# Turning 32x32 diagonal blocks on the vector engine in place of two trips through DRAM, in a DeltaNet and mixer kernel

## The chip, the cores and the metric

The kernel runs on one core of a Trainium2 chip. The metric is the time of one execution on that core in microseconds (us), as the median of several executions. A run is called faster or slower when it differs by more than 2%, and unclear when the interval reaches across that line. Every ratio quoted below is the mean time of one kernel's runs over the mean time of the other kernel's runs of the same rounds, so it is not quite the ratio of the medians that stand beside it. The kernel before has two medians below: 850.98 us from its first three runs, 851.62 with a fourth.

Engine names in the profile: PE is TensorE (matmuls), DVE is VectorE, ACT is ScalarE, POOL is GpSimd, SP is SyncE, which issues most DMAs. The *granted clock* is the TensorE clock allowed in a stretch, as the profile gives it, as a share of full speed (0.50 to 1.00 in the windows of the prediction). An *eviction* is the copy that takes a matmul's result out of its accumulator, and a *hole* is a long stretch in which PE stands idle.

## The reference

```python
# q, k, v: (4, 8, 768, 48); beta: (4, 8, 768)
k_n = k / (norm(k) + 1e-6)
for t in range(S):                               # DeltaNet, per batch and head
    y[t]  = q[t] @ state
    v_old = k_n[t] @ state
    state = state + beta[t] * outer(k_n[t], v[t] - v_old)
# then, per batch, a mixer on x = (768, 384):
u   = x + (relu(x.T @ w_tok1) @ w_tok2).T
out = u + relu(u @ w_ch1) @ w_ch2
```

The kernel does the recurrence in chunks of 64 tokens. In each chunk the chain of updates becomes a triangular 64x64 system for each head, and its inverse is built from two 32x32 diagonal blocks and one block between them.

## The kernel before

A *unit* is 128 tokens of one batch (two chunks, eight heads, so 16 triangular systems); there are 24 units, six for each batch. For a unit, `prep` makes the masked products `gm`. Its 32 diagonal 32x32 blocks (two for each system) lie with the row on the partition. `invert` wants one whole block on each partition, so that VectorE can invert up to 128 blocks at once by 60 small instructions (0.37 us each in the trace). The change of layout goes through DRAM, out and back. A *round* is the set of units inverted together; there are seven. The code counts them from zero, so "rounds two and later" are the third to the seventh; they are called the later rounds here. `join` completes the 64x64 inverse and `recur` walks the chunks.

```python
rounds = [[0, 1], [2, 3, 4, 5]]                  # then four units each

def prep(u):
    ...                                          # transposes, kqt and kbd copies
    for g in range(2):                           # p_g: key-query products
        ...
        nc.vector.tensor_tensor(out=gm[:, r, 0::2], in0=p_g, in1=mb..., op=ALU.mult)
    for par in range(2):                         # first trip, out
        for i in range(2):
            nc.sync.dma_start(
                out=xins[rnd][lo : lo + NB].rearrange("b s t -> s b t"),
                in_=gm[row : row + HB, :, 2, HB * i : HB * i + HB])

def invert(rnd):
    nc.sync.dma_start(out=x, in_=xins.pop(rnd)[0:n])         # first trip, back
    for s in range(1, HB - 1):
        nc.vector.tensor_tensor(out=tmp, ..., op=ALU.mult)
        nc.vector.tensor_tensor(out=x[:, 0:s, s + 1 : HB], ..., in1=tmp, op=ALU.add)
    nc.vector.memset(...)                                    # ones on the diagonal
    nc.sync.dma_start(out=w_dram[0:n], in_=x)                # second trip, out

def fetch_w(u):                                              # second trip, back
    nc.sync.dma_start(out=wt[row : row + HB, :, HB * i : HB * i + HB],
                      in_=w_dram[lo : lo + NB].rearrange("b s t -> s b t"))

def join(u):
    nc.vector.transpose(t11[...], wt[r, :, 0:HB])
    ...  # p_z = gm block x t11, copied to zst; p_x = zst x wt, copied into wt

def recur(t):
    # p_q = s_bd x kqt      -> r_bd = v - p_q  (VectorE)
    # p_w = wt x r_bd       -> w_bd            (ScalarE)
    # p_s = gm x w_bd       -> s_bd, y         (VectorE)
    ...
```

A plan gives every piece of work a time, and the instructions are emitted in that order, so each engine's stream is fixed when the kernel is built. The build still reorders a little: e5 below keeps the plan, and yet its instructions run in another order on every engine. The mixer of a batch runs beside the recurrence of the next.

## Time and profile before

| quantity | before |
|---|---|
| median time | 850.98 us (850.45 to 856.06) |
| span in the trace | 850.4 us |
| first p_z (first join) | 84.9 us |
| first matmul of the first mixer | 202.2 us |
| from there to the end | 648.2 us |
| busy share PE, DVE, ACT | 86%, 46%, 30% |

How to read it: the first matmul of the mixer (out `p`, in `xb` and `w`) divides the span. Before it, PE waits for the preparation; after it, PE is almost full (busy 490.45 of the 500.40 us from 350 us on) and the recurrences of the later batches run between mixer matmuls. I use two numbers: the *mixer start* and the *rest*. They add up to the span.

The prediction shows the slices, the windows and the waits before the mixer start. One more view is needed later: what PE waited for *after* it, on behalf of the recurrence. The columns of a wait line are the waiting engine and matmul, what ended the wait, the us in all, the number of waits, and the longest. Kernel before, waits of PE in 202.2 to 850.4 us:

```profile
PE p_z L413 <- DVE t L407: 3.2, 3, 2.3
PE p_q L453 <- DVE s_bd L486: 2.5, 2, 1.5
PE p_w L470 <- DVE r_bd L455: 1.6, 3, 0.6
```

With two further waits (0.4 us for p_z, 0.2 us for p_s) that is 7.9 us in 648: the later rounds, with their DRAM trips, stand almost entirely beside other work.

### The profile page before, as it was taken

To read this page: it belongs to the slowest core of one execution; us is meant where nothing else is said; L and a number is where in the kernel's file an instruction comes from. 1 tells how busy PE (TensorE), PEld (TensorE's weight loads), DVE (VectorE), ACT (ScalarE), POOL (GpSimd) and SP (SyncE) were. 2 spreads that over 40 slices of the span, in tenths; PEclk is the share of its full clock that TensorE was granted. 3 is DMA by queue.
4 is the path that set the end of the run, shared out by engine and by line. 5 is a ranking of instruction groups with operands and counts; after the bars stand their busy time and mean duration, and the time that the engine had idled before them with its cause. 6 is when DMAs were issued, how large, how long until landed. Compare 5 with 4: busy or idle time off the path is not lost.

```text
span 850.4 us, 13384 instructions
## 1 busy us (share of the span) xinstructions
PE 732.3 (86%) x5080; PEld 606.6 (71%) x5080; DVE 394.8 (46%) x1081; ACT 253.0 (30%) x596; POOL 111.6 (13%) x142
## 2 busy tenths in 40 slices
PE   5630654969689999999999899999999999999998
PEld 4620644856469797887787888886898888678876
DVE  4487775756973459333267323493229422010000
ACT  5430422744234522333231333311332222111110
POOL 4322112223430211002000001110000000000000
PEclk9765755987899999999999999999999999999999
DMA  7763414445433441224122223202110200000000
GB/s 137 138 144 63 107 28 126 71 82 155 121 109 53 71 94 24 68 44 78 29 48 54 43 49 69 46 19 53 22 39 20 44 11 10 9 1 20 11 9 19
DMA packets 164591, 49.73 MB, mean 58 GB/s; under 512 B 155536, under 2 KB 158608, under 8 KB 164528
## 3 DMA queue, kind: packets, MB, share of 16 engines
q1 hardware_dynamic: 164480, 48.79, 26.6%
q8 instruction: 40, 0.66, 0.3%
q14 instruction: 23, 0.19, 0.1%
q10 hardware_dynamic: 48, 0.10, 0.0%
HBM read 37.85 MB, written 11.01 MB: 57 GB/s over the span
## 4 chain that ended last, share of the span: by engine, by line
PE 49%; DVE 9%; DMA 2%; ACT 2%; issue 1%; SPq 1%; ACTq 0%
PE p_c L549 16%; PE p_o L564 15%; DVE x L377 3%; DVE sub L373 3%; PE p_h L523 3%; PE p_s L482 2%; PE p_g L338 2%; PE p_q L453 2%; PE p L510 2%; PE p_w L470 2%; PE p_x L422 1%; PE p_z L413 1%; SPq L251 1%; PE p_ut L533 1%; DMA kst<-in_k_dram 1%
## 5 line engine op out<-in xcount | busy, mean ns | idle before, releaser
L549 PE MATMUL p_c<-u_t,wc 128*128 128x128 f32 x1728 | 218.2, 280 | 2.5 <-ACT u_t L537 1.8
L549 PEld LDWEIGHTS p_c<-u_t,wc 128*128 128x128 f32 x1728 | 206.5, 195 | 7.8 <-ACT u_t L537 2.5
L564 PE MATMUL p_o<-wc,r 128*128 128x384 f32 x576 | 197.5, 490 | 3.1 <-DVE wc L195 3.1
L564 PEld LDWEIGHTS p_o<-wc,r 128*128 128x128 f32 x576 | 105.0, 191 | 64.8 <-DVE wc L195 4.4
L556 ACT ACTIVATE r<-p_c 128x512 f32<-128x512 f32 x72 | 43.0, 597 | 156.8 <-PE p_c L549 156.4
L373 DVE TENSOR_TENSOR sub<-x 128x84 f32<-128x84 f32 (+22 forms) x210 | 77.3, 368 | 22.9 <-DMA x<-n_dram 18.3
L377 DVE TENSOR_TENSOR x<-x,sub 128x84 f32<-128x84 f32 (+22 forms) x210 | 76.7, 365 | 4.7
L338 PE MATMUL p_g<-kqt,kbd 128*128 128x128 f32 x384 | 60.1, 313 | 17.9 <-ACT kqt L326 17.7
L413 PE MATMUL p_z<-t,gm 128*65 128x64 f32 x384 | 30.7, 236 | 50.2 <-DVE t L407 49.8
L338 PEld LDWEIGHTS p_g<-kqt,kbd 128*128 128x128 f32 x384 | 55.1, 223 | 24.0 <-ACT kqt L326 22.5
L570 DVE TENSOR_TENSOR xb<-xb,p_o 128x384 f32<-128x384 f32 x24 | 13.3, 554 | 116.2 <-PE p_o L564 116.0
L413 PEld LDWEIGHTS p_z<-t,gm 128*65 128x65 f32 x384 | 28.7, 151 | 52.7 <-issue 28.5
L486 DVE TENSOR_TENSOR s_bd<-s_bd,p_s 64x192 f32<-64x192 f32 (+1 forms) x100 | 31.6, 316 | 73.9 <-PE p_s L482 72.2
L482 PE MATMUL p_s<-w_bd,gm 128*128 128x96 f32 x384 | 58.5, 297 | 5.2 <-ACT w_bd L474 4.9
L482 PEld LDWEIGHTS p_s<-w_bd,gm 128*128 128x128 f32 x384 | 52.6, 208 | 10.3 <-ACT w_bd L474 9.1
L340 DVE TENSOR_TENSOR gm<-p_g,mb 128x512 f32<-128x512 f32 x48 | 33.0, 690 | 57.3 <-PE p_g L338 55.0
L453 PE MATMUL p_q<-s_bd,kqt 128*128 128x96 f32 x352 | 50.9, 287 | 4.2 <-DVE s_bd L486 3.9
L453 PEld LDWEIGHTS p_q<-s_bd,kqt 128*128 128x128 f32 x352 | 47.1, 201 | 9.6 <-issue 3.0
L470 PE MATMUL p_w<-r_bd,wt 128*65 128x96 f32 x384 | 45.5, 263 | 7.2 <-issue 3.5
L455 DVE TENSOR_TENSOR r_bd<-v_st,p_q 64x192 f32<-64x192 f32 (+1 forms) x110 | 34.8, 316 | 35.1 <-PE p_q L453 23.0
L459 ACT ACTIVATE xb<-p_q 64x384 f32<-64x384 f32 (+1 forms) x55 | 23.0, 419 | 92.7 <-DVE r_bd L455 92.4
L474 ACT COPY w_bd<-p_w 64x192 f32<-64x192 f32 (+1 forms) x120 | 33.5, 280 | 54.0 <-PE p_w L470 52.0
(70 smaller groups left out, 708.8 us busy)
## 6 DMA issues: line engine op xcount, KB each, us to landing
d<-in_moe_w_ch_dram SPq DMA_DIRECT2D x24, 384.0 KB, 3.3
kpad<-in_k_dram SPq DMA_DIRECT2D x24, 192.0 KB, 3.5
kst<-in_k_dram SPq DMA_DIRECT2D x96, 48.0 KB, 2.6
qpad<-in_q_dram SPq DMA_DIRECT2D x24, 192.0 KB, 3.6
v_st<-in_v_dram SPq DMA_DIRECT2D x96, 48.0 KB, 2.6
out_dram<-xb SPq DMA_DIRECT2D x24, 192.0 KB, 1.9
n_dram<-gm SPq DMA_DIRECT2D x96, 32.0 KB, 1.7
wt<-w_dram SPq DMA_DIRECT2D x96, 32.0 KB, 2.1
```

The lines of the kernel that those rows point to most:

```text
L338: nc.tensor.matmul(p_g[:, i], kbd[:, nb], kqt[:, nb])
L373: nc.vector.tensor_tensor(out=tmp, in0=x[:, 0:s, s : s + 1].to_broadcast([n, s, w]), in1=x[:, s : s + 1, s + 1 : HB].to_broadcast([n, s, w ...
L377: nc.vector.tensor_tensor(out=x[:, 0:s, s + 1 : HB], in0=x[:, 0:s, s + 1 : HB], in1=tmp, op=ALU.add,)
L413: nc.tensor.matmul(p_z[0:65, nb], gm[:, lo : lo + 65], t11[:, nb])
L453: nc.tensor.matmul(p_q[:, p], kqt[:, 2 * p + cc], s0[:, p])
L455: nc.vector.tensor_tensor(out=r_bd[r, hp, e], in0=v_st[r, hp, cc], in1=p_q[hi, hp, e], op=ALU.subtract,)
L470: nc.tensor.matmul(p_w[0 : C + 1, p], wts[u % NW][:, w_lo : w_lo + C + 1], r_bd[:, p])
L474: nc.scalar.copy(w_bd[r, hp, e], p_w[lo, hp, e])
L482: nc.tensor.matmul(p_s[:, p], gm[:, 2 * p + cc, 0:2], w_bd[:, p])
L549: nc.tensor.matmul(p_c[:, i], wc1[:, cb, f * 128 : (f + 1) * 128], u_t[:, cb], start=(cb == 0), stop=(cb == NCB - 1),)
L556: nc.scalar.activation(r, p_c, ACTF.Relu)
L564: nc.tensor.matmul(p_o, r2[f // FG][:, f % FG], wc2[:, f], start=(f == 0), stop=(f == NHT - 1),)
```

## The change

The intent: do the change of layout on the chip. Four copies a unit put the diagonal blocks into a `turned` tile, one VectorE instruction (STREAM_TRANSPOSE in the trace, 1.97 us for 128x1024) transposes its 32x32 blocks, and the inverse comes back the same way into the place of the masked block in `gm`. With that, the first round takes four units, so that one long wait for an inversion goes away.

```diff
-    rounds = [[0, 1], [2, 3, 4, 5]]
+    rounds = [[0, 1, 2, 3], [4, 5]]
 ...
+    turned = const.tile([128, HB, RU * NB], FP32, name="turned")
 # prep(u), at its end
-                nc.sync.dma_start(out=xins[rnd][...].rearrange("b s t -> s b t"), in_=gm[...])
+        for block, t in quarters(u):
+            nc.scalar.copy(t, block)
 # quarters(u): for the four 32-row quarters r
+            yield (gm_of(u)[r, :, 2, cols],
+                   turneds[rnd][r, :, lo : lo + NB].rearrange("s t b -> s b t"))
 # invert(rnd)
-        nc.sync.dma_start(out=x, in_=xins.pop(rnd)[0:n])
+        nc.vector.transpose(x.rearrange("b s t -> b t s"), turned)
 ...
-        nc.sync.dma_start(out=w_dram[0:n], in_=x)
+        nc.vector.transpose(turned, x.rearrange("b s t -> b t s"))
+        for u in rounds[rnd]:
+            for i, (block, t) in enumerate(quarters(u)):
+                if u < NCH and i % 2:
+                    nc.vector.tensor_copy(out=block, in_=t)
+                else:
+                    nc.scalar.copy(block, t)
-    def fetch_w(u): ...                          # gone, with the wt tiles
 # the key loads of the first four units move from SyncE's to ScalarE's queue
-                stacked(kst, k, u)
+                stacked(kst, k, u, nc.scalar if u < NK else nc.sync)
 # plan of the first round
-                at(-3.5 + 0.3 * j, 0.06, prep, u)
+                at(-3.7 + 0.3 * j, 0.06, prep, u)
 ...                                              # and of the inversions
```

Cut: a scaling moved from GpSimd to VectorE in the first round, a fourth key buffer, the load of beta moved to SyncE, the in-place square in the weight rounding, merged tiles, a second `turned` tile borrowed for the second round, and the other plan times. Note the layout of `turned`: index `t` outside, block index inside. A copy of one unit's quarter therefore writes (or reads) one element in every 32, a step of 128 bytes.

More of the change, by code (lines that the diff above doesn't have):

```diff
@@ L80 @@
     )
-    dram = ctx.enter_context(
-        tc.tile_pool(name="dram", bufs=2, space=bass.MemoryType.DRAM)
-    )
     def ps_prep(shape, name):
@@ L112 @@
     NV = 6
-    NW = 3
-    NK = 3
+    NK = 4
     kpad = tiles("kpad", [128, H, DP], NK)
@@ L120 @@
     GW = 3 * DP
-    gms = tiles("gm", [128, NB * GW + 8], NV)
+    gm_all = const.tile([128, NV * NB * GW + 8], FP32, name="gm")
+    gmb = gm_all[:, 0 : NV * NB * GW].rearrange("s (b n) -> s b n", n=GW)
     kqts = tiles("kqt", [128, NB, 2, C], NV)
     nrms = tiles("nrm", [128, NP, 2], NV)
-    wts = tiles("wt", [128, NB * C + 8], NW)
-    t11s = tiles("t11_", [128, NB, 2 * HB], 2)
+    t11 = const.tile([128, NB, 2 * HB], FP32, name="t11")
+    turned = const.tile([128, HB, RU * NB], FP32, name="turned")
     zst = const.tile([128, NB * 2 * HB + 8], FP32, name="zst")
@@ L136 @@
     nc.vector.memset(kbd, 0.0)
-    for t in gms:
-        pad = t[:, 0 : NB * GW].rearrange("s (b three n) -> s b three n", b=NB, n=DP)
-        nc.vector.memset(pad[:, :, 1, D:DP], 0.0)
-        nc.gpsimd.memset(t[:, NB * GW :], 0.0)
-    for t in t11s + wts + [zst]:
+    nc.vector.memset(gmb[:, :, DP + D : 2 * DP], 0.0)
+    nc.gpsimd.memset(gm_all[:, NV * NB * GW :], 0.0)
+    for t in [t11, zst, turned]:
         nc.gpsimd.memset(t, 0.0)
@@ L155, in load_beta @@
         rows = mlp_pool.tile([B * H, S], FP32, name="b_rows", tag="xb")
-        nc.scalar.dma_start(out=rows, in_=beta.rearrange("b h s -> (b h) s"))
+        nc.sync.dma_start(out=rows, in_=beta.rearrange("b h s -> (b h) s"))
         yield
@@ L181, in round_weights @@
         f = loads.tile([128, WP], U32, name="w_f")[:, 0:n]
-        a = loads.tile([128, WP], FP32, name="w_a")[:, 0:n]
         nc.scalar.activation(lo, lo, ACTF.Copy, scale=2.0**-29)
-        nc.scalar.square(a, hi.bitcast(FP32))
         nc.vector.tensor_scalar(
@@ L192, in round_weights @@
         )
+        a = hi.bitcast(FP32)
+        nc.scalar.square(a, a)
         nc.gpsimd.tensor_tensor(out=f, in0=f, in1=lo, op=ALU.add)
@@ L218 @@
     ksts = {}
-    xins = {}
-    xouts = {}
-    rounds = [[0, 1], [2, 3, 4, 5]]
+    rounds = [[0, 1, 2, 3], [4, 5]]
     while rounds[-1][-1] < NU - 1:
@@ L226 @@
     turning = set()
+    masked = set()
+    inverted = set()
     walked = set()
@@ L237, in load_kq @@
         b, c = divmod(u, NCH)
-        ksts[u] = kst = loads.tile([128, NP, 2, D], FP32, name="kst")
+        ksts[u] = kst = loads.tile([128, NP, 2, D], FP32, name="kst", bufs=NK)
         for pad, src in ((kpad, k), (qpad, q)):
@@ L244, in load_kq, with stacked @@
             if src is k:
-                stacked(kst, k, u)
-    def stacked(dst, src, u):
+                stacked(kst, k, u, nc.scalar if u < NK else nc.sync)
+    def stacked(dst, src, u, queue):
         rows = heads_of(src, u)
@@ L250, in stacked @@
             for cc in range(2):
-                nc.sync.dma_start(
+                queue.dma_start(
                     out=dst[C * par : C * par + C, :, cc], in_=rows[par, cc]
@@ L256, in load_v @@
         vsts[u] = v_st = loads.tile([128, NP, 2, D], FP32, name="v_st")
-        stacked(v_st, v, u)
+        stacked(v_st, v, u, nc.sync)
         yield
@@ L270, in gm_of, with weights_of @@
     def gm_of(u):
-        return gms[u % NV][:, 0 : NB * GW].rearrange(
-            "s (b three n) -> s b three n", three=3, n=DP
-        )
-    def wt_of(u):
-        return wts[u % NW][:, 0 : NB * C].rearrange("s (b n) -> s b n", n=C)
+        return gmb[:, (u % NV) * NB : (u % NV + 1) * NB].rearrange(
+            "s b (three n) -> s b three n", n=DP
+        )
+    def weights_of(u, nb):
+        lo = ((u % NV) * NB + nb) * GW + 2 * DP
+        return gm_all[:, lo : lo + C + 1]
     def prep(u):
@@ L316, in prep @@
         mb = work.tile([128, NP, 2, C], FP32, name="mb", bufs=1)
-        nc.gpsimd.tensor_tensor(
+        scaler = nc.vector if u in rounds[0] else nc.gpsimd
+        scaler.tensor_tensor(
             out=mb, in0=mask_c[:, None, None, :].to_broadcast([128, NP, 2, C]),
@@ L326, in prep @@
         nc.scalar.mul(kqt_q, p_t, -1.0)
-        nc.gpsimd.tensor_tensor(
+        scaler.tensor_tensor(
             out=gm[:, :, 1, 0:D].rearrange("s (p c) d -> s p c d", c=2), in0=kst,
@@ L347, in prep, with turn_for, quarters @@
             yield
+        if round_of[u][1] == 0:
+            turn_for(round_of[u][0])
+        for block, t in quarters(u):
+            nc.scalar.copy(t, block)
         turning.remove(u)
-        rnd, j = round_of[u]
-        if j == 0:
-            xins[rnd] = dram.tile([RU * 4 * NB, HB, HB], FP32, name="n_dram")
-        for par in range(2):
-            for i in range(2):
-                lo = (4 * j + 2 * par + i) * NB
-                row = C * par + HB * i
-                nc.sync.dma_start(
-                    out=xins[rnd][lo : lo + NB].rearrange("b s t -> s b t"),
-                    in_=gm[row : row + HB, :, 2, HB * i : HB * i + HB],
-                )
-        yield
-    def invert(rnd):
-        n = 4 * NB * len(rounds[rnd])
-        x = work.tile([RU * 4 * NB, HB, HB], FP32, name="x", bufs=1)[0:n]
-        nc.sync.dma_start(out=x, in_=xins.pop(rnd)[0:n])
+        masked.add(u)
+    turneds = {}
+    def turn_for(rnd):
+        if rnd == 1:
+            turneds[rnd] = mlp_pool.tile([128, HB, RU * NB], FP32, name="xb", tag="xb")
+            nc.gpsimd.memset(turneds[rnd], 0.0)
+        else:
+            assert not set(turneds) - {1}
+            turneds[rnd] = turned
+    def quarters(u):
+        rnd, j = round_of[u]
+        lo = j * NB
+        for i in range(4):
+            r = slice(HB * i, HB * i + HB)
+            cols = slice(HB * (i % 2), HB * (i % 2) + HB)
+            yield (
+                gm_of(u)[r, :, 2, cols],
+                turneds[rnd][r, :, lo : lo + NB].rearrange("s t b -> s b t"),
+            )
+    def invert(rnd):
+        n = 128
+        assert masked.issuperset(rounds[rnd])
+        turned = turneds[rnd]
+        x = work.tile([n, HB, HB], FP32, name="x", bufs=1)
+        nc.vector.transpose(x.rearrange("b s t -> b t s"), turned)
         yield
@@ L370, in invert @@
             w = HB - 1 - s
-            tmp = work.tile([RU * 4 * NB, HB * HB // 4], FP32, name="sub")
+            tmp = work.tile([n, HB * HB // 4], FP32, name="sub")
             tmp = tmp[0:n, 0 : s * w].rearrange("b (s w) -> b s w", w=w)
@@ L382, in invert @@
         nc.vector.memset(x.rearrange("b s t -> b (s t)")[:, 0 :: HB + 1], 1.0)
-        xouts[rnd] = w_dram = dram.tile([RU * 4 * NB, HB, HB], FP32, name="w_dram")
-        nc.sync.dma_start(out=w_dram[0:n], in_=x)
-        yield
-    def fetch_w(u):
-        assert u < NW or u - NW in walked
-        rnd, j = round_of[u]
-        w_dram, wt = xouts[rnd], wt_of(u)
-        for i in range(2):
-            for par in range(2):
-                lo = (4 * j + 2 * par + i) * NB
-                row = C * par + HB * i
-                nc.sync.dma_start(
-                    out=wt[row : row + HB, :, HB * i : HB * i + HB],
-                    in_=w_dram[lo : lo + NB].rearrange("b s t -> s b t"),
-                )
+        nc.vector.transpose(turned, x.rearrange("b s t -> b t s"))
[3 more added lines that the diff above has]
+                    nc.vector.tensor_copy(out=block, in_=t)
+                else:
+                    nc.scalar.copy(block, t)
+        del turneds[rnd]
+        inverted.update(rounds[rnd])
+        yield
     def join(u):
-        gm, wt = gms[u % NV], wt_of(u)
-        t11 = t11s[u % 2]
+        assert u in inverted
+        wt = gm_of(u)[:, :, 2]
         for par in range(2):
@@ L411, in join @@
         for nb in range(NB):
-            lo = nb * GW + 2 * DP
-            nc.tensor.matmul(p_z[0:65, nb], gm[:, lo : lo + 65], t11[:, nb])
+            nc.tensor.matmul(p_z[0 : C + 1, nb], weights_of(u, nb), t11[:, nb])
         z = zst[:, 0 : NB * 2 * HB].rearrange("s (b n) -> s b n", n=2 * HB)
@@ L468, in recur @@
             for p in range(p0, p1):
-                w_lo = (2 * p + cc) * C
                 nc.tensor.matmul(
-                    p_w[0 : C + 1, p], wts[u % NW][:, w_lo : w_lo + C + 1], r_bd[:, p]
+                    p_w[0 : C + 1, p], weights_of(u, 2 * p + cc), r_bd[:, p]
                 )
@@ L610 @@
             if rnd == 0:
-                at(-3.5 + 0.3 * j, 0.06, prep, u)
+                at(-3.7 + 0.3 * j, 0.06, prep, u)
             elif rnd == 1:
-                at(-2.7 + 0.4 * j, 0.06, prep, u)
+                at(-1.9 + 0.7 * j, 0.12, prep, u)
             else:
                 at(max(t0 - 3.0 + 0.3 * j, start(u - NV + 1) + 0.01), 0.06, prep, u)
-            at(start(u) - 0.45, 0, fetch_w, u)
             at(start(u) - 0.3, 0.1, join, u)
         if rnd == 0:
-            at(-2.7, 2.0 / (HB + 2), invert, rnd)
+            at(-2.4, 2.0 / (HB + 2), invert, rnd)
         elif rnd == 1:
-            at(-0.4, 1.9 / (HB + 2), invert, rnd)
+            at(0.1, 3.2 / (HB + 2), invert, rnd)
         else:
```

## The prediction

> **What bounds the kernel now.** I first read the 40 slices of the page, because the busy shares of the whole span (PE 86%, DVE 46%, ACT 30%) mix stages with different limits.
>
> ```profile
> PE   5630654969689999999999899999999999999998
> DVE  4487775756973459333267323493229422010000
> PEclk9765755987899999999999999999999999999999
> DMA  7763414445433441224122223202110200000000
> ```
>
> A slice is 21.3 us. From slice 12 on (about 250 us) TensorE is full at full clock; only the first twelve slices have room. So I cut the span at the places where the kind of work changes, with the windows view (columns: stretch, length, busy us and instruction count of PE, PE weight loads, DVE, ACT and POOL, granted clock, DMA share, GB/s):
>
> ```profile
> 0.00:48.40 48.40, 29.15 (x176) 25.70 (x176) 22.33 (x67) 23.42 (x50) 19.90 (x42) 0.82 0.74 140
> 48.40:78.70 30.30, 3.71 (x16) 3.48 (x16) 28.95 (x83) 5.60 (x12) 6.09 (x7) 0.58 0.47 96
> 78.70:90.60 11.90, 3.93 (x33) 3.71 (x33) 5.25 (x16) 1.74 (x6) 3.83 (x7) 0.50 0.70 170
> 90.60:119.20 28.60, 20.02 (x124) 17.50 (x124) 21.96 (x74) 11.71 (x37) 3.17 (x3) 0.68 0.22 49
> 119.20:145.50 26.30, 6.78 (x53) 6.15 (x53) 18.52 (x56) 5.68 (x14) 7.41 (x7) 0.50 0.40 103
> 145.50:183.20 37.70, 33.89 (x301) 31.11 (x299) 24.84 (x76) 23.52 (x67) 9.80 (x11) 0.96 0.42 71
> 183.20:202.20 19.00, 11.91 (x64) 10.75 (x65) 9.38 (x30) 7.25 (x22) 2.21 (x3) 0.58 0.51 132
> 202.20:252.00 49.80, 37.78 (x153) 24.91 (x153) 44.85 (x120) 17.51 (x37) 20.90 (x20) 0.91 0.39 114
> 350.00:850.40 500.40, 490.45 (x3415) 401.68 (x3413) 164.18 (x422) 122.63 (x274) 27.43 (x33) 1.00 0.15 32
> ```
>
> In order: preparation of six units; the first inversion (DVE 29 of 30 us); its results through DRAM and the first join; four recurrence steps beside the second inversion; waiting for the end of that inversion and its DRAM trip; six steps; a wait and two more steps. At 202.2 the first mixer starts, and from there the span is TensorE's: about 648 us with only about 25 us idle. The PE waits up to 202 us, and the places in PE's order of time, say what ends each hole:
>
> ```profile
> PE p_z L413 <- DVE t L407: 46.6, 2, 28.1
> PE p_g L338 <- ACT kqt L326: 17.2, 7, 7.2
> PE p_x L422 <- DMA wt<-w_dram: 6.2, 1, 6.2
> ```
> ```profile
> 84.91 1.99 PE L413 MATMUL p_z<-t,gm 128*65 128x64 f32 x16 [28.11 <-DVE t L407]
> 139.27 2.02 PE L413 MATMUL p_z<-t,gm 128*65 128x64 f32 x16 [18.53 <-DVE t L407]
> 190.70 1.94 PE L422 MATMUL p_x<-wt,zst 128*65 128x32 f32 x16 [6.24 <-DMA wt<-w_dram]
> ```
>
> The two large holes are named after a small transpose, but what they wait for is an inversion plus a DRAM trip. From the DVE timeline: the last step of inversion 0 ends at 78.7 and p_z starts at 84.9; that of inversion 1 ends at 131.3 and p_z starts at 139.3. So two DRAM returns of 6.2 and 8.0 us, and the 6.2 us hole at 190.7, where the third wt buffer came free late. The inversion itself is
>
> ```profile
> L373 DVE TENSOR_TENSOR sub<-x 128x84 f32<-128x84 f32 (+22 forms) x210 | 77.3, 368 | 22.9 <-DMA x<-n_dram 18.3
> L377 DVE TENSOR_TENSOR x<-x,sub 128x84 f32<-128x84 f32 (+22 forms) x210 | 76.7, 365 | 4.7
> ```
>
> seven rounds of 60 instructions at 0.37 us: 22 us of DVE each, whether for 64 or 128 partitions.
>
> [...] here the median landing is 1.7 us (n_dram), 2.6 (w_dram), 2.1 (wt)[...]. [...] the sync queue pays about 0.65 us per kst issue, and that will now be ScalarE's time. [...] The new copies step 128 bytes per element; no group of the kernel before does that, so their time is my least known size.
>
> **The change part by part.**
> 1. *DRAM trips go*: 96 n_dram and 96 wt issues with 128-byte rows, 7+7 whole-tile ones. On the path: the 6.2 and 8.0 us returns and the 6.2 us buffer hole. In their place: [...] 8 copies on DVE (8 x 0.36 = 2.9 us, with 8 on ScalarE beside them), then the same small transposes: about 4.5 us. Gross saving near 12 us if nothing else moved.
> 2. *Round one has four units.* The inversion costs the same 22 us, but units 2 and 3 no longer wait for a second one. In return the first may start only when four units are masked, and the order of instructions built from the changed kernel shows more put inside it: 13 pieces of weight rounding (five token, eight channel) against about four before.
> 3. *ScalarE gets 8 copies per unit*, 0.36 us each if like the 32x256 copies of L417: 24 x 8 x 0.36 = 69 us, less 12 moved to DVE in the first six units. In the preparation four of them stand between the mask of one unit and the block-diagonal copies of the next: the 6.5 us between units becomes about 7.5.
> 4. *16 kst loads on ScalarE's queue at the start*: by the order they come ahead of its first copy. About 2.4 MB must be under way by then; at 140 GB/s, less what may be in flight, ScalarE is free at about 13 us, where its first kqt copy began at 10.4 before. Scaling by VectorE instead of POOL (0.69 + 0.54 against 1.06 + 0.88 us) gives some of that back.
>
> The timeline, by hand. First unit masked at about 20 us (16.9 before), the fourth at 42 to 43, copies 1.5, transpose: the first step of inversion 0 at about 46 (48.4 before, where it also stood behind other DVE work). In it: 22 us of steps, 13 x 1.27 = 16.5 us of weights (0.35+0.54+0.54 less overlap), 2.4 of masks, 2.6 of sums and small ones[...]: 46, so an end at about 92 (78.7 before). Chains and copies: p_z at 97 (84.9), first step at 103 (90.6). Inversion 1 then runs beside the steps of units 0 to 3: 22 of steps, 20 of recurrence (7 x 3.1 less 2), 3 of joins, 3 of weights[...], 5 of waits: 55 from 95.5, to 150. Step 8 ends at about 159. Units 4 and 5 are four steps at 6 us with the preparations of units 6 to 9 beside them (37.7/6 = 6.3 a step before, ScalarE now near its limit there): the mixer starts at about 183 to 185, against 202.2, a gain of 18. After that the same 648 us, in which inversion 2 and eleven weight pieces meet again (DVE 44.85 of 49.8 us before, so no large gain), plus 3 us because bursts of 16 ScalarE copies (5.8 us) stand ahead of ReLU evictions in four rounds: 184 + 648 + 3 = 835. I choose 836, one above, for the stepped copies.
>
> **Rivals.**
> *A: The gain is the whole hole.* If the weight pieces fit the DVE gaps and the four-unit round ends at 80, the mixer would start near 172 and the span be about 822. For it: both holes together are 46.6 us and the plan has been retuned. Against it: DVE was 29 of 30 us busy in inversion 0 already; there are no gaps.
> *B: ScalarE becomes the bound.* If the stepped copies take twice 0.36 us, a burst is 11 us, a preparation 9 us, and each of four bursts stalls TensorE some 4 us: about 855. For it: everything in the mixer passes through ScalarE in order. Against: ACT is only 25% busy after 350 us, and TensorE has other work ready.
> *C: Hidden weights come due.* The rounding DMAs are paced by three buffers, each now held until the last DVE use. If inversion 0 stalls on them (8 us per turn of a buffer, 2.7 us per piece, 13 pieces are 35 us against 46), it doesn't; with DMA at 140 GB/s it might by 5 to 8 us: about 842.
>
> **Range and chances.** A and B are each perhaps one in seven, C one in four. Range 819 to 855. The 2% line is 834, just below my number: faster 0.43, same 0.53, slower 0.04.
>
> **What would show it.** Right: no n_dram or w_dram; p_z first at 95 to 99 us and no second hole of 18 us; the mixer (L520) first at 180 to 188; [...] inversion 0 about 45 us long with DVE near full; about 650 us from mixer to end. Wrong: an inversion 0 ending before 85 (A), ScalarE copies of 0.6 us or more with PE waiting for ACT after 350 us (B), DVE waiting for weight DMAs inside inversion 0 (C), or the fourth unit masked after 50 us (the start mis-sized).

What is cut above rested on rules and figures that no trace of this case shows, among them my estimate for one of the new 128x1024 transposes. Its terms are cut from three sums, whose totals stand: about 4.5 us in part 1 (printed now: 2.9 us of copies and the small transposes), 46 us for inversion 0 (the printed terms make 43.5) and 55 us for inversion 1 (53). The forecast came to 184 + 648 + 3 = 835, put at 836. Three more sizes are estimates: ScalarE free at 13 us, from the 140 GB/s of the first window and about 2.4 MB of loads; 0.36 us for VectorE's copies, from ScalarE's L417 (363 ns); and C's 8 us for a turn of a buffer, of which the trace of the kernel before shows 7.1 (3.3 us from issue to landing and 3.8 in the six instructions of a piece). Measured on VectorE before the change are 433 ns for a 32x256 transpose and 690 ns for a 128x512 tensor_tensor; the key loads took a median of 0.61 us each on SyncE's queue.

## The result and the profile after

| | before | after |
|---|---|---|
| median | 851.62 us (850.45 to 856.06, 4 runs) | 890.64 us (887.59 to 896.34, 4 runs) |
| ratio | | 1.0456, 95% interval 1.0391 to 1.0521 |
| span in the trace | 850.4 us | 894.5 us |
| first p_z | 84.9 us | 111.5 us |
| mixer start | 202.2 us | 221.9 us |
| mixer start to end | 648.2 us | 672.6 us |

The kernel became slower by 4.6%, where 836 us had been predicted. In the traces it loses 19.7 us before the mixer start and 24.4 us after it. These sum to 44.1 us where the medians differ by 39.0, because the profiled run of the changed kernel (896.34 us) was the slowest of its four.

The DRAM trips did go (DMA bytes fell from 49.7 to 37.1 MB), the second hole of 18 us went too, and the result is correct. The slices of the page, PE and ACT of the changed kernel (each digit tenths of busy time, 22.4 us each):

```profile
PE   3551097777968997899998899999999999999998
ACT  2664442584356642525443426526252422110110
```

PE has one long hole in place of two, but afterwards it has 7s and 8s where it had 9s. The groups of the changed kernel (out and in, shape, count, busy us, mean ns, idle time just before them and what ended it):

```profile
L350 ACT COPY turned<-gm 32x256 f32<-32x256 f32 x88 | 55.6, 632 | 29.5 <-DVE gm L339 28.6
L408 ACT COPY gm<-turned 32x256 f32<-32x256 f32 x80 | 50.2, 627 | 16.5 <-DVE turned L402 15.2
L386 DVE STREAM_TRANSPOSE x<-turned 128x1024 f32<-128x1024 f32 x6 | 11.8, 1970 | 10.2 <-ACT turned L350 10.2
```

The copies take 0.63 us, not 0.36; the transposes 1.97 us, more than my estimate, which no trace had shown. The preparation shows it: the first key-query products start at 17.8, 28.8, 38.2 and 47.8 us, intervals of 9.4 to 11.0 where they had been 6.2 to 6.9. The waits of PE in 0 to 221.9 us:

```profile
PE p_z L424 <- DVE t L419: 36.7, 1, 36.7
PE p_g L337 <- ACT kqt L325: 27.0, 9, 5.1
```

The p_z holes fell from 46.6 to 36.7 us, as intended, but p_g now waits 27.0 us for ScalarE (17.2 before). And after the mixer start, the waits of PE for the recurrence in the changed kernel:

```profile
PE p_z L424 <- ACT gm L408: 8.1, 2, 5.4
PE p_s L492 <- ACT w_bd L484: 7.9, 4, 3.1
PE p_w L480 <- DVE r_bd L466: 7.5, 7, 2.4
PE p_q L464 <- DVE s_bd L496: 4.9, 5, 1.5
PE p_x L433 <- ACT zst L428: 1.9, 2, 1.6
```

Together 30.3 us, where the kernel before had 7.9. Two spots show how such a wait comes about. First ScalarE's and PE's order of time around 355 us (start, us, engine, line, operation, count, idle before and its releaser):

```profile
355.44 10.19 ACT L408 COPY gm<-turned 32x256 f32<-32x256 f32 x16 [2.00 <-DVE turned L402]
365.66 0.65 ACT L484 COPY w_bd<-p_w 64x192 f32<-64x192 f32 x2
```
```profile
353.08 0.85 PE L480 MATMUL p_w<-r_bd,gm 128*65 128x96 f32 x8 [0.65 <-DVE r_bd L466]
358.02 2.02 PE L424 MATMUL p_z<-t,gm 128*65 128x64 f32 x16 [2.74 <-ACT gm L408]
366.36 0.91 PE L492 MATMUL p_s<-w_bd,gm 128*128 128x96 f32 x6 [2.83 <-ACT w_bd L484]
```

The p_w product is done at 353.9 us, but its copy to w_bd starts at 365.66, because sixteen copies of an inversion that this step doesn't need stand in front of it on ScalarE. PE fills most of the time with other work, but stalls 2.74 us for the first of these copies (p_z belongs to the join of the next unit) and 2.83 us for w_bd, which stands behind the last. Second, VectorE around 484 us:

```profile
483.90 0.36 DVE L466 TENSOR_TENSOR r_bd<-v_st,p_q 64x192 f32<-64x192 f32 x1
484.18 1.89 DVE L402 STREAM_TRANSPOSE turned<-x 128x1024 f32<-128x1024 f32 x1
486.10 0.36 DVE L466 TENSOR_TENSOR r_bd<-v_st,p_q 64x192 f32<-64x192 f32 x1
```
```profile
486.61 0.85 PE L480 MATMUL p_w<-r_bd,gm 128*65 128x96 f32 x8 [2.39 <-DVE r_bd L466]
```

The big transpose falls between the two halves of r_bd, and p_w waits 2.39 us. Lastly, what ScalarE itself stood waiting for in 221.9 to 894.5 us, before copies that the change added:

```profile
ACT turned L350 <- DVE gm L339: 25.5, 11, 4.2
ACT gm L408 <- DVE turned L402: 14.4, 5, 4.2
```

The trips had waited on SyncE's queue, where loads and stores stand behind them but no eviction of the recurrence. The copies wait on ScalarE, where the evictions do.

### The profile page after: what moved, and what is told of

Same layout as the page of the kernel before. It is cut to its first block, busy times and chain, and to the rows that moved or that the text cites. A ratio compares the mean times of both kernels' runs of the same rounds, so it can differ in the third digit from the quotient of the medians. Undisturbed runs are those within 1.5% of the kernel's fastest.

```text
span 894.5 us, 13280 instructions
## 1 busy us (share of the span) xinstructions
PE 753.1 (84%) x5080; PEld 622.8 (70%) x5080; DVE 428.6 (48%) x1112; ACT 364.0 (41%) x775; POOL 104.3 (12%) x127
## 4 chain that ended last, share of the span: by engine, by line
PE 56%; DVE 19%; ACT 10%; issue 3%; DMA 1%; POOL 1%; SPq 0%; ACTq 0%; POOLq 0%; DVEq 0%
PE p_o L574 16%; PE p_c L559 14%; PE p_s L492 5%; DVE x L396 4%; DVE sub L392 4%; PE p_g L337 3%; ACT gm L408 3%; PE p_w L480 3%; PE p_q L464 3%; PE p_h L533 3%; PE p L520 3%; PE p_x L433 2%; ACT turned L350 2%; PE p_z L424 2%; DVE r_bd L466 1%
## 5 line engine op out<-in xcount | busy, mean ns | idle before, releaser
L559 PEld LDWEIGHTS p_c<-u_t,wc 128*128 128x128 f32 x1728 | 203.9, 192 | 7.1 <-ACT u_t L547 1.8
L574 PEld LDWEIGHTS p_o<-wc,r 128*128 128x128 f32 x576 | 108.0, 195 | 64.4 <-issue 3.9
L396 DVE TENSOR_TENSOR x<-x,sub 128x30 f32<-128x30 f32 (+14 forms) x210 | 77.5, 369 | 4.3
L392 DVE TENSOR_TENSOR sub<-x 128x30 f32<-128x30 f32 (+14 forms) x210 | 76.0, 362 | 4.4
L492 PE MATMUL p_s<-w_bd,gm 128*128 128x96 f32 x384 | 63.3, 308 | 12.3 <-ACT w_bd L484 12.2
L424 PE MATMUL p_z<-t,gm 128*65 128x64 f32 x384 | 35.2, 254 | 44.9 <-DVE t L419 36.7
L492 PEld LDWEIGHTS p_s<-w_bd,gm 128*128 128x128 f32 x384 | 55.9, 218 | 17.6 <-ACT w_bd L484 16.7
L350 ACT COPY turned<-gm 32x256 f32<-32x256 f32 x88 | 55.6, 632 | 29.5 <-DVE gm L339 28.6
L424 PEld LDWEIGHTS p_z<-t,gm 128*65 128x65 f32 x384 | 33.3, 169 | 47.1 <-issue 37.4
L464 PEld LDWEIGHTS p_q<-s_bd,kqt 128*128 128x128 f32 x352 | 49.2, 209 | 14.4 <-issue 8.0
L480 PE MATMUL p_w<-r_bd,gm 128*65 128x96 f32 x384 | 47.1, 268 | 13.4 <-DVE r_bd L466 12.2
L408 ACT COPY gm<-turned 32x256 f32<-32x256 f32 x80 | 50.2, 627 | 16.5 <-DVE turned L402 15.2
```

What stands on the lines that cost most here:

```text
L350: nc.scalar.copy(t, block)
L392: nc.vector.tensor_tensor(out=tmp, in0=x[:, 0:s, s : s + 1].to_broadcast([n, s, w]), in1=x[:, s : s + 1, s + 1 : HB].to_broadcast([n, s, w ...
L396: nc.vector.tensor_tensor(out=x[:, 0:s, s + 1 : HB], in0=x[:, 0:s, s + 1 : HB], in1=tmp, op=ALU.add,)
L408: nc.scalar.copy(block, t)
L424: nc.tensor.matmul(p_z[0 : C + 1, nb], weights_of(u, nb), t11[:, nb])
L464: nc.tensor.matmul(p_q[:, p], kqt[:, 2 * p + cc], s0[:, p])
```

## The experiments

Sixteen kernels ran. They are told in groups, not quite in the order in which they ran. The table gives the medians and what the traces show; *waits* is the sum of PE's waits for p_z, p_x, p_w, p_q and p_s after the mixer start (waits named "issue" left out).

| kernel | median us | ratio to before | mixer start | rest | waits |
|---|---|---|---|---|---|
| before | 850.98 | 1 | 202.2 | 648.2 | 7.9 |
| after | 890.64 | 1.0456 | 221.9 | 672.6 | 30.3 |
| e1 plain copies | 857.29 | 1.0118 | 204.6 | 650.1 | 20.0 |
| e2 key loads on SyncE | 885.84 | 1.0429 | 208.1 | 673.8 | 28.5 |
| e3 rounds as before | 889.99 | 1.0477 | 216.8 | 671.5 | 29.1 |
| e4 late copies on GpSimd | 869.12 | 1.0229 | 209.0 | 657.7 | 22.7 |
| e5 copies cut to 1/32 | 858.67 | 1.009 | 203.9 | 653.3 | 17.3 |
| e6 before, four units | 849.36 | 1.001 | 203.4 | 643.9 | 6.6 |
| e7 plain, all on VectorE | 861.99 | 1.013 | 199.6 | 660.1 | 20.9 |
| e8 plain, GpSimd late | 851.68 | 1.0005 | 196.8 | 655.9 | 15.7 |
| e9 flat transposes | 922.91 | 1.0842 | 221.7 | 700.2 | 48.0 |
| e10 VectorE, then ScalarE | 852.40 | 1.0007 | 199.9 | 651.5 | 17.9 |
| e11 VectorE, then GpSimd | 852.78 | 1.0019 | 193.2 | 656.5 | 20.5 |
| e12 plain, key loads on SyncE | 854.17 | 1.004 | 196.0 | 656.0 | 16.0 |
| e13 VectorE, then trips | 840.12 | 0.9889 | 187.9 | 651.0 | 3.4 |
| e14 plain ScalarE, then trips | 829.10 | 0.976 | 184.6 | 642.7 | 4.7 |
| e15 changed, then trips | 842.02 | 0.9903 | 201.7 | 639.3 | 5.1 |
| e16 e14, key loads on ScalarE | 834.28 | 0.9819 | 194.1 | 639.8 | 4.8 |

### e1: the step taken out of the copies

```diff
-    turned = const.tile([128, HB, RU * NB], FP32, name="turned")
+    turned = const.tile([128, RU * NB, HB], FP32, name="turned")
-                turneds[rnd][r, :, lo : lo + NB].rearrange("s t b -> s b t"),
+                turneds[rnd][r, lo : lo + NB],
-        nc.vector.transpose(x.rearrange("b s t -> b t s"), turned)
+        nc.vector.transpose(x.rearrange("b s t -> b t s"), turned.rearrange("s b t -> s t b"))
```

The step moves from the copies to the big transposes, which have a stepped side anyway. The order of instructions is the same on every engine as in the changed kernel, so this is a clean test of cost.

> One edit of the changed kernel: the tile between masks and transposes is laid out block by block instead of column by column, so the ScalarE copies are contiguous and the two 128x1024 transposes are stepped on both sides. The order of instructions on every engine stays the same. Theory T (the copies stepping 128 bytes, 0.63 us each instead of 0.36, cost most of the 40 us): copies fall to about 0.42 us (a plain 128x256 ScalarE copy takes 0.43), ScalarE loses some 38 us of busy time, transposes stay near 2 us, and the time falls by 10 to 15 us, to 875 to 880. Rival S (the start: four units in round one, key loads issued by ScalarE, cost it): copies get shorter but the time stays within 4 us of the changed kernel, about 888.

Measured: 857.29 us (ratio 1.0118, 1.0075 to 1.0162). The group of copies in this kernel:

```profile
L412 ACT COPY gm<-turned 32x256 f32<-32x256 f32 x80 | 32.2, 402 | 16.6 <-DVE turned L404 15.3
```

402 ns in place of 627, and 33 us of time by the medians (29 by the two ratios), far more than the 10 to 15 that I had expected. The traces put 17 before the mixer start and 22 after; they differ by 39.8 us, as the changed kernel's is of its slowest run. The transposes stayed at 1.99 and 1.96 us. So the step of the copies costs some 30 us *in this arrangement*. But 20.0 us of recurrence waits remain, and the kernel is still not faster than the one before.

### e2, e3, e6: the smaller parts of the change

```diff
# e2
-                stacked(kst, k, u, nc.scalar if u < NK else nc.sync)
+                stacked(kst, k, u, nc.sync)
# e3: rounds and plan times of before, everything else as changed
-    rounds = [[0, 1, 2, 3], [4, 5]]
+    rounds = [[0, 1], [2, 3, 4, 5]]
# e6: kernel before with the changed rounds, plan times, NW = 4 and in-place square
-    rounds = [[0, 1], [2, 3, 4, 5]]
+    rounds = [[0, 1, 2, 3], [4, 5]]
```

> One edit of the changed kernel: the first sixteen key loads go back to the sync queue. Rival S: ScalarE's first copy comes at about 10.5 instead of 14.6 us, the fourth unit is masked 4 to 5 us earlier, and the time falls by as much, to about 885. Theory T: the same few us at most, since the interval of 9.5 us between units has nothing to do with the loads; 885 to 892.

> The changed kernel with the rounds and the plan times of the kernel before (two units in round one, four in round two); the layout change stays. Theory T: the first join comes again near 88 us, the mixer starts within 8 us of where it did before (202), but the stretch from mixer to end keeps its extra 20 us or more: 868 to 878. Rival S: without the four-unit round most of the loss is gone: 852 to 860.

> The kernel before (DRAM trips, no copies) with the four-unit first round and its plan times alone; to fit, one more inverse buffer and the in-place square of the weights, which frees the room. Theory T: the first join late by some 20 us, but one hole less, so 850 to 862, and the stretch from mixer to end stays at about 648 us. Rival S: 865 to 875, as the four-unit round is what costs.

Measured: e2 885.84 us, with the first p_g at 14.4 us in place of 17.8; so about 5 us by the medians, as expected, but only 2 by the ratios, whose intervals overlap. e3 889.99 us: the second hole is back (p_z at 147.2 us after a wait of 15.8 us), but p_z comes first at 95.3 us in place of 111.5, and the sum is the same. What was expected of e3 by both theories missed. e6 849.36 us, ratio 1.001, and rival S (865 to 875) missed: one long hole of 46.4 us in place of two, and no gain. So making the first round of four units is neutral in both settings. As I read it, the holes are VectorE's inversion work, and merging the rounds only moves it; no run tests that by itself.

### e4, e5, e7, e9: shorter copies, other engines, flat transposes

```diff
# e4: copies of the later rounds
-            nc.scalar.copy(t, block)
+            if round_of[u][0] > 1: nc.gpsimd.tensor_copy(out=t, in_=block)
+            else:                  nc.scalar.copy(t, block)      # and the same on the way back
# e5: ScalarE's copies move one column of 32 (the result is wrong on purpose)
+            nc.scalar.copy(t[:, :, 0:1], block[:, :, 0:1])
# e7: e1 and e2, and every copy nc.vector.tensor_copy
# e9: the inverse tile is stored transposed, so both big transposes are without a step
-        nc.vector.transpose(x.rearrange("b s t -> b t s"), turned)
+        x = xt.rearrange("b t s -> b s t"); nc.vector.transpose(xt, turned)
```

> The changed kernel (stepped copies) with the copies of rounds two and later on POOL instead of ScalarE. Theory T (bursts of 16 stepped copies on ScalarE stall TensorE in the mixers): the stretch from the mixer's start to the end falls from 672 to 650 to 660 us, and as four of the copies before the mixer move too, the whole to 865 to 876. Rival: if the mixer's extra 24 us come from the transposes or the in-place inverse, the stretch stays at 668 or more. How long POOL takes for a stepped 32x256 copy is not known; if it is over 2 us, this turns into a new wait.

> The changed kernel with each ScalarE copy cut to one column of eight blocks (32x8 elements in place of 32x256): a wrong result on purpose, all waits kept, only the copies' length taken away, to some 0.2 us each. Theory T: 835 to 850, at or a little below the plain-copy version and near the kernel before. Rival: another cost of the change, 10 us or more, stays, and the time is over 860.

> The plain-copy layout, key loads on the sync queue, and all copies on VectorE (0.29 us each there in the plain-copy run, against 0.40 on ScalarE). Theory T: ScalarE is again as free as in the kernel before; preparation intervals fall below 7.5 us; VectorE gains some 55 us of work, most of it where it has room; 832 to 848. Rival (VectorE becomes the bound before the mixer and late in the inversions): 850 to 862.

> The changed kernel with the inverse computed on a transposed tile, so that both 128x1024 transposes read and write contiguously and the steps of the inversion are stepped in its place; the copies stay stepped. [...] if it is their size or the 128 partitions, they stay at 1.9 or more. The inversion steps stay at 0.37 us if stepping costs VectorE arithmetic nothing. Whole time within 5 us of the changed kernel's 888 in either case.

(From e9's text a size for a transpose without a step is cut, which no run had shown by then. It asked whether the transposes' 1.97 us come from the step or from their size.)

Measured: e4 869.12, e5 858.67 (relative error 1.007, as intended wrong), e7 861.99, e9 922.91 us. In e4, e5, e7 and e9 the built order of instructions differs from the changed kernel's, so none is as clean as e1. e4's theory held in time and rest; of e7's two ranges the rival's (850 to 862) held, at its edge.

e5 was the surprise: ScalarE's copies fell to 0.20 us, half of a plain copy, and the kernel was no faster than with plain ones (858.67 against 857.29). I had expected 835 to 850. So, as far as a kernel with another built order can tell, my theory that the *length* of the copies is the whole cost had to be given up: something about turning on the engines costs time even when the copies are short. e7 (VectorE) and e4 (GpSimd, still stepped, 0.63 us) say that it isn't ScalarE alone either: with the copies elsewhere the rest was 660.1 and 657.7 us. But for stepped copies ScalarE is a worse place than GpSimd: moving the late ones there brought 21.5 us back.

e9 settles the size of the transposes. Its groups:

```profile
L387 DVE STREAM_TRANSPOSE x<-turned 128x1024 f32<-128x1024 f32 x6 | 7.5, 1246 | 10.2 <-ACT turned L350 10.2
L393 DVE TENSOR_TENSOR sub<-x 128x30 f32<-128x30 f32 (+14 forms) x210 | 101.3, 482 | 4.4
```

Without a step the transpose takes 1.25 us; with it, in the changed kernel, 1.97. But the step then sits in the 420 inversion instructions, whose mean goes from 0.36 to 0.48 us (0.37 to 0.48 for the other half), some 48 us of VectorE for ten saved. 32 us were lost against the changed kernel, where I had expected no more than 5 either way and steps of 0.37 us.

### e8, e10, e11, e12: the best placements with the turning kept everywhere

```diff
# all four: e1 (plain) and e2 (key loads on SyncE), and
# e12: nothing else                     e8: later rounds on GpSimd
# e10: first two rounds on VectorE, later ones on ScalarE
# e11: first two rounds on VectorE, later ones on GpSimd
```

> Plain layout of the turned blocks (copies without a step), the key loads issued by SyncE, and from the third inversion round on the copies on GpSimd. Theory (ScalarE's time is what the change spends): ScalarE is relieved in both stretches, so the mixer starts at about 200 us as the plain layout alone gave 204.6 with the key loads still on ScalarE, and mixer to end falls from the plain layout's 650 to the 644 to 648 that the kernel with the DRAM trips shows: 842 to 851 us. Rival (GpSimd is a worse place for the late copies, as its copies of 32x256 elements took 0.63 us in the stepped run against 0.62 on ScalarE, and it has to wait behind its own work on the expert weights): mixer to end stays at 655 to 660: 853 to 862 us.

> Plain layout, key loads on SyncE, and the copies of the first two inversion rounds (six units) on VectorE, the later ones on ScalarE. The run with all copies on VectorE had its first p_z at 91.6 us and its mixer start at 199.6 us, and lost its gain after the mixer's start (660 us to the end). Theory (the copies must stand on whichever engine has slack in that stretch: VectorE before the first inversion, ScalarE after): first p_z at 91 to 93, mixer start at 198 to 201, mixer to end 650 as in the plain layout alone: 844 to 852 us. Rival (the time after the mixer's start grows by what was won before it, since weights and streams come due there): 852 to 860 us.

> As the run before it in this list, with the later copies on GpSimd in place of ScalarE. If the late stretch is bound by ScalarE (kernel w_bd and gm waits), mixer to end falls under 650 and the time is 838 to 847 us; if GpSimd's copies only bring a later wait of their own (p_z behind gm by GpSimd, 7 us in the stepped run), 852 to 862 us.

> Plain layout and key loads on SyncE, nothing else: the sum of the two single edits. They gave -33 us and -5 us against the changed kernel each alone. If they add, 851 to 855 us, with the first key-query product at 14.3 us and the first p_z at 100 us; if the key loads' 3.5 us are absorbed by VectorE's inversion chain or by the mixer, 855 to 859 us, no different from the plain layout alone.

Measured: 851.68, 852.40, 852.78 and 854.17 us against 851.59 for the kernel before in the same rounds; ratios 1.0005 to 1.004. All four start the mixer earlier than the kernel before, by 2 to 9 us, and all four lose it again afterwards: rests of 651.5 to 656.5 us and recurrence waits of 15.7 to 20.5 us. With plain copies, moving them from one engine to another doesn't help in the later rounds. The rivals of e10 and e11 held, both at the edge of their ranges; e8's rival held in its rest (655.9 us), while its time lies between the two ranges. e12's two edits added up in time.

### e13 and e14: the turning in the first two rounds only

If the later rounds are the place of loss, putting their trips back and leaving the first two rounds changed should give the early mixer start *and* the undisturbed rest.

```diff
# prep(u), invert(rnd), plan
+        if rnd >= 2:                              # as before the change
+            nc.sync.dma_start(out=xins[rnd][lo : lo + NB].rearrange("b s t -> s b t"), in_=block)
+        else:
+            for block, t in quarters(u): ...copy(t, block)
 ...
+            if rnd >= 2: at(start(u) - 0.45, 0, fetch_w, u)    # lands in the masked block's place
# plain copies, key loads on SyncE; copies on VectorE (e13) or ScalarE (e14)
```

> Hybrid: the first two inversion rounds (six units) turn by 32x32 transposes, with plain copies on VectorE, and key loads on SyncE, as in the run that had its mixer start at 193 to 200 us; the five later rounds go through DRAM as before the change, but land in the masked block's place. Theory (given back in the later rounds through the engine time of transposes and copies on the recurrence's path): mixer start 193 to 200 us, mixer to end 644 to 649 us as in the two kernels with trips: 838 to 848 us. Rival (a start won early is lost later in any case): mixer to end 651 to 656 us and 849 to 854 us in all.

> The same hybrid with the copies of the first two rounds on ScalarE, plain, as in the run that had its mixer start at 196.0 us and 656.0 us from there to the end. Theory: mixer start 195 to 198 us, mixer to end 644 to 649 us: 840 to 847 us. Rival: mixer to end 652 to 657 us and 850 to 854 us in all.

Measured: e13 840.12 us (ratio 0.9889, 0.9865 to 0.9913), e14 **829.10 us** (0.976, 0.9734 to 0.9786). e14 beats both kernels, and by more than I had expected (840 to 847); it is the only one of the sixteen that counts as faster than the kernel before. By the 2% rule e13 and e15 count as the same, though their intervals lie below 1, and e4 and e16 are unclear. In e14 the mixer starts at 184.6 us and the rest is 642.7 us. e13 met the expected time, but not by the expected division: its rest was 651.0 us, though its recurrence waits were only 3.4 us; PE there waited 10.9 us for channel weights instead, which VectorE, busy with the copies of the early rounds, rounds late by then (that cause is read from the trace, not tested). Against e10, its counterpart with turning everywhere, e13 gained 12 us, all before the mixer start: the rests are 651.0 and 651.5 us. So fewer recurrence waits did not shorten the rest there.

### e15 and e16: which edit carries it

```diff
# e15: the changed kernel with trips in the later rounds, nothing else
#      (stepped copies and key loads on ScalarE stay)
# e16: e14 with the key loads on ScalarE as in the changed kernel
```

> The changed kernel with the DRAM trips back in the five later inversion rounds; stepped copies and the key loads on ScalarE stay in the first two. Theory (the late turning costs some 27 us after the mixer's start and part of the 20 us before it, since round two's copies fall in that stretch): mixer start 205 to 215 us, mixer to end 642 to 649 us, 850 to 862 us. Rival (what the stepped copies delay early is carried to the end, or the trips help only together with plain copies): mixer to end over 655 us, 868 us or more.

> The hybrid with plain copies on ScalarE and DRAM trips in the five later rounds, with the key loads of the first four units left on ScalarE's queue as the change has them. If the key loads cost what they did in the changed kernel (5 us), 832 to 837 us, first key-query product at 17.9 us in place of 14.9 us; if VectorE's chain hides it, 828 to 831 us.

Measured: e15 842.02 us (0.9903, 0.9861 to 0.9945), e16 834.28 us (0.9819, 0.9778 to 0.9859). So with the 0.63 us copies left in the first two rounds, the trips in the later ones alone bring the changed kernel from 890.6 to 842.0 us: more than the whole loss, and below the 850 to 862 us that I had expected. The waits of PE after the mixer start in e15:

```profile
PE p_z L460 <- DVE t L455: 1.9, 2, 1.4
PE p_q L500 <- DVE s_bd L532: 1.5, 1, 1.5
PE p_w L516 <- DVE r_bd L502: 1.4, 2, 0.9
PE p_s L528 <- ACT w_bd L520: 0.3, 1, 0.3
```

5.1 us in place of 30.3. The windows of the two kernels from mixer start to end (length; busy us of PE, PE weight loads, DVE, ACT, POOL with counts; granted clock, DMA share, GB/s), first the changed kernel, then e15:

```profile
221.92:894.50 672.58, 630.45 (x4321) 513.27 (x4320) 267.28 (x659) 248.58 (x506) 51.02 (x57) 0.98 0.11 26
```
```profile
201.72:841.00 639.28, 618.51 (x4322) 505.51 (x4320) 258.14 (x679) 171.93 (x385) 55.12 (x62) 1.00 0.19 42
```

Of the 33.3 us, PE's idle time accounts for 21.4 (42.1 against 20.8) and its busy time for 11.9: practically the same matmuls at a granted clock of 0.98 in place of 1.00. ScalarE is rid of 77 us.

Of the 20.2 us by which e15's mixer starts earlier, 14.2 lie in units 4 and 5 (29.2 us from the end of step 8, the last of units 0 to 3, against 43.4). The other 6.0 lie earlier, where PE, VectorE, ScalarE and GpSimd still run the same instructions in the same order in both kernels (in the changed one until 177 us), so I don't count them as the edit's work. The granted clock differs there, as the windows of 118 to 162 us show, first the changed kernel (0.56), then e15 (0.75):

```profile
118.00:162.00 44.00, 36.18 (x218) 32.77 (x216) 30.97 (x102) 16.49 (x55) 5.88 (x6) 0.56 0.20 41
```
```profile
118.00:162.00 44.00, 33.73 (x250) 30.36 (x248) 34.72 (x120) 18.07 (x59) 5.67 (x6) 0.75 0.21 43
```

The 6.0 us are about what the changed kernel's profiled run lay above its median (5.7). So a mixer start from a single trace is uncertain by some us.

The four corners, medians in us:

| | turning in all rounds | trips in the later rounds |
|---|---|---|
| stepped copies | 890.64 (after) | 842.02 (e15) |
| plain copies | 857.29 (e1) | 834.28 (e16) |

The step costs 33 us where the later rounds turn too, and 8 us where they don't. Turning the later rounds costs 49 us with stepped copies and 23 with plain ones. The two losses are not separate: most of the step's price is paid in the later rounds. (The corners come from three calls. By the ratios to the kernel before of their own rounds, 1.0456, 1.0118, 0.9903 and 0.9819, the four differences are about 29, 7, 47 and 25 us, the same picture. One more thing differs: in e16 all copies are on ScalarE, while in the other three 12 of the early ones are on VectorE. With early copies on VectorE, e10 against e13, the later turning cost 12 us.)

## Why the prediction was wrong

**The direction of the whole.** 836 us were predicted, 890.6 came. The mixer start was predicted at 183 to 185 us and came at 221.9; the rest was predicted at 651 us (648 plus 3) and came at 672.6. Both terms failed. Of the 38 us at the mixer start, 12 were there before the first step of inversion 0 (57.9 us in place of 46), and some 19 came in units 4 and 5. The two inversions themselves took what was predicted: 46.7 and 55.4 us, against 46 and 55.

**The step that failed most: turning the later rounds was taken to cost next to nothing.** The prediction gave them "plus 3 us because bursts of 16 ScalarE copies (5.8 us) stand ahead of ReLU evictions in four rounds", and the preparations of units 6 to 9 nothing beyond "ScalarE now near its limit there". In place of 3 us the rest grew by 24.4 us. In the stretch of units 4 and 5, where 24 us were predicted for four steps, the changed kernel's step 8 ended at about 178.5 us and the mixer started at 221.9: 43 us. e15 shows it by doing the later rounds the old way: 29 us for the same stretch, and a rest of 639.3 us. As I read the trace, what I missed isn't the number of copies but what stands behind them; no run separates the two. I had set them against ReLU evictions, for which PE has other work (it waited 0.2 us in all for ReLU's results after the mixer start). In the trace they stand ahead of w_bd and zst, links of the recurrence's chain, and the transposes stand between the halves of r_bd.

**The mis-sized term: the stepped copy.** 0.36 us was taken from copies of the same size that read PSUM (L417, 363 ns); measured are 0.63 us, and 0.40 us without the step (e1); for the twelve copies on VectorE 0.37 and 0.29 us. With it the preparation took 9.4 to 11.0 us a unit, and the fourth unit was masked at 52.3 us: the prediction's own sign "after 50 us". Four copies of 0.63 on the 6.5 us of before are 9.0; even the prediction's 0.36 makes 7.9, not the 7.5 that it used. Nor did the way from the last inversion step to p_z get shorter: 6.9 us, against 6.2 with the DRAM return and 5 predicted (4.9 in e14, with plain copies). The prediction named this its "least known size", added one microsecond for it, and asked in rival B what twice 0.36 would do. B had the right sign: copies of 0.6 us or more and PE waiting for ACT after 350 us are exactly what the trace shows. But B came to 855 only: it named a preparation of 9 us too, but the only stall that it priced was some 4 us at each of four bursts.

**The four-unit round.** Merging was taken to save a hole. The hole went (one wait of 36.7 us in place of 46.6), but e3 and e6 show the merge as neutral. Where e14's gain over the kernel before comes from is open in part. Beside e6, which has the same rounds with trips, e14's rest is alike (642.7 against 643.9 us), and so is the end of step 8 (153.7 against 154.8). Its 18.8 us lie in units 4 and 5 (30.9 against 48.6), where e6 waits 6.45 us for the join of unit 5 and from 150 us to the mixer start has a granted clock of 0.74, e14 0.91. How much belongs to the second round's missing return, to the inverse in the masked block's place, which spares the wt buffers, or to the scaling on VectorE and the fourth key buffer was not tested alone.

**Smaller terms.** The 128x1024 transposes: 1.97 us, as their rearranged side is stepped, against 1.25 without the step (e9); the prediction's size for them was my estimate, not shown by a trace. ScalarE free at 13 us: its first kqt copy began at 15.3, and the key loads are worth about 5 us by the medians (e2; 834.28 against 829.10 for e16 and e14), little more than the noise. The first p_z followed at 111.5 rather than 97. Rival C (weights come due) did not show: DVE was busy 45 of 49 us inside inversion 0.

**What was right.** The hand-made timeline of the front part was not a bad one for cheap copies: e14 starts the mixer at 184.6 us with a first p_z at 94.2 (183 to 185 and 97 predicted). That is one agreement in a sum, and partly luck: e14's inversion 0 took 41.0 us (46 predicted) and its units 4 and 5 took 30.9 (24 predicted), errors that nearly cancel.

**What stays open.** With plain copies the later turning still costs some 23 us, and neither shorter copies (e5) nor another engine (e7, e8, e11) removed it; with early copies on VectorE it is 12 us, none of them in the rest (e10, e13). The trace shows two ways, ScalarE or VectorE held by turning work in front of the recurrence. I did not separate the share of the transposes, of the copies' own waits (25.7 and 14.5 us of ScalarE standing idle before them in e1, as in the changed kernel) and of the later arrival of the inverse. All edits but e1 also alter the built order of instructions.

## What to carry to other kernels

In this kernel the hidden DMA round trips cost next to nothing (7.9 us of waits in 648), while engine instructions in their place cost the engines' time and delayed what stood behind them in their streams (a w_bd copy from 353.9 to 365.66 us). So look first where a wait for a trip is on the path, replace those (here two rounds of seven, 2.4% faster), and leave the hidden ones. Before adding instructions to an engine with low average load, look in the timeline at what follows them there: in the changed kernel, after the mixer start, PE waited 7.9 us for w_bd, an eviction of the recurrence chain, and 0.2 us for those of the mixer's ReLU, a throughput stage. When a layout puts a step somewhere, put it into the few instructions where it costs least: here the fourteen transposes (1.97 us against 1.25), not the 192 copies (on ScalarE 0.63 against 0.40) and not the 420 inversion steps (0.48 against 0.36).
